# Windowed attention with a gated MLP: the first pair is transposed and brought out ahead of the branch, and the raw tiles of the third and fourth pair get places of their own

## The chip, the cores and the metric

One Trainium2 chip, one core of it. The metric is the time of the program on the device in microseconds (us), the median of several runs. Five engines work side by side, each through a list of its own in order: PE (TensorE, matrix products and transposes), DVE (VectorE), ACT (ScalarE), POOL (GpSimd) and SP (SyncE, which here issues nearly all DMAs). They wait for each other by semaphores.

## What is computed

q, k and v are float32 of shape 4 x 8 x 768 x 64 (batches, heads, positions, head size). Each head does attention in a band: a position sees the `n_sink` = 4 first positions and the last `window` = 128. The result, 4 x 768 x 512, goes through an MLP with a convolution over three positions and a gate; its weights come as 64-bit floats.

```python
scores = scale * np.matmul(q, k.transpose(0, 1, 3, 2))
keep = is_sink | in_window
scores = np.where(keep, scores, -1000000000.0)
a = np.exp(scores - np.max(scores, axis=-1, keepdims=True))
a = a / (np.sum(a, axis=-1, keepdims=True) + 1e-09)
x = np.matmul(a, v)                      # then heads side by side: 768 x 512
h = np.maximum(x @ w_in, 0.0)
conv_out = sum(conv_w[k] * hp[:, k:k + S, :] for k in range(3))   # hp: h, padded
out = h / (1.0 + np.exp(-conv_out)) @ w_out
```

## The kernel before

**The start.** SP loads the two scalars and the first four raw tiles: q and k of the first half (three tiles of 128 positions) of pair 0 and pair 1 (`raw`, L401). A *pair* is two heads, whose head sizes fill the 128 rows; there are 16 pairs, `g` 0 to 15, four a batch. DVE works out from the scalars whether band and sinks fit the fast path (`flag`, L874 to L876) and makes mask pieces (L896 to L902). All engines then load the flag and branch (L904, L906): `banded` if it is 1, `general` if not. Here it is 1.

**In the branch.** DVE makes the masks `m0`, `w1` and `w2` (L470 to L478), POOL fills zeros, the sinks' place `vs` and small tiles. Then a loop runs over steps: for the first batch all four pairs' first halves, then all second halves (24 steps of one query tile each), then pair by pair. In a step, PE multiplies the queries `X` with the keys `kk`/`kks` of the tile and its neighbour (`sc`, L378), DVE adds the mask and reduces (L577), ACT takes the exponent (L580), DVE sums and inverts (L583, L584), POOL scales (L586), PE transposes the result (L603), ACT copies it out (`pT`, L605), and PE multiplies with v (`px`, L655).

**Pairs of the first batch** come in plain float32: `prep32` has PE transpose a raw tile of q or k (`trq`, `trk`, L357) and ACT bring it out: q twice with `headscale` into `X`, k once into `kks` (L288), sinks beside it (L366). The four buffers `raw` are used in turn; `fetch` asks for the next load only when a transpose has been asked for, so that the load of pair 2's q goes where pair 0's q was.

**The weights** (`wi_0r` and so on, 512 KB each) come in the same loop: ACT starts with a scaled copy of the high words (`stm`, L118), DVE puts the bits together (L121 to L123), POOL and DVE split the result in a high and a low part (L130, L131). `WHEN` says at which step each is due; three buffers hold raw weights. From step 12 on, the MLP's products (`ph` L204, `po` L239) are laid between the steps.

The order on each engine is fixed ahead of the run by a scheduler from priorities and waits. SP's list is in order too, so a DMA that waits for its buffer holds back those behind it.

## Time and profile before

| | |
|---|---|
| median of 3 runs | 475.0 us (472.65 to 475.37) |
| the profiled execution | 473.48 us |
| its span, first to last instruction | 471.8 us |
| PE busy | 444.6 us (94%) |
| DVE busy | 339.0 us (72%) |
| ACT busy | 321.3 us (68%) |
| POOL busy | 281.3 us (60%) |
| chain that ended last | PE 75%, DVE 11%, ACT 4%, POOL 3%, DMA 2% |

The shares are averages over stages with different limits, so they are read by stages below. A row of the timeline gives start and duration in us, then engine, line, operation, what is written and read, and the count of merged instructions; in square brackets stands how long the engine was idle before it and what ended the wait. Issues of DMAs on SP show the time the issue took, not the flight.

### The profile page before, as it was taken

The page shows a single profiled execution, that of the slowest core. Times are in us where ns is not written, and L with a number is a line of the kernel's source. Part 1 is how long each engine was busy: PE and PEld are TensorE (multiplying, and loading weights), DVE is VectorE, ACT ScalarE, POOL GpSimd, SP SyncE. Part 2 cuts the span into 40 slices and gives each one's busy share as a digit, 9 for nine tenths or more (in the row PEclk, how much of TensorE's full clock was granted, in tenths as well). Part 3 has the DMA queues.
Part 4 walks back from the last instruction along what each step waited for, and adds up shares of the span by engine and source line. Part 5 has one row for each costly group of instructions (what it writes and reads, how often), then busy time and mean ns, then how long its engine had stood idle before and what let it go on. Part 6 is the DMA issues. An engine that isn't in the chain of part 4 may idle for free.

```text
span 471.8 us, 10560 instructions
## 1 busy us (share of the span) xinstructions
PE 444.6 (94%) x3181; PEld 388.3 (82%) x3181; DVE 339.0 (72%) x1190; ACT 321.3 (68%) x1027; POOL 281.3 (60%) x557
## 2 busy tenths in 40 slices
...
GB/s 140 219 229 251 183 201 107 81 199 203 167 153 179 137 175 68 161 146 133 61 192 81 166 119 134 143 120 124 71 141 15 46 1 46 0 23 24 24 24 53
DMA packets 105851, 55.91 MB, mean 119 GB/s; under 512 B 83072, under 2 KB 98712, under 8 KB 105784
## 3 DMA queue, kind: packets, MB, share of 16 engines
...
q10 hardware_dynamic: 144, 0.13, 0.1%
...
## 4 chain that ended last, share of the span: by engine, by line
PE 75%; DVE 11%; ACT 4%; POOL 3%; DMA 2%; issue 2%; DVEq 0%; POOLq 0%; ACTq 0%
PE ph L204 26%; PE po L239 25%; PE px L655 7%; PE sc L382 3%; PE sc L381 3%; PE pts L617 3%; PE px L678 2%; DVE stm L122 2%; PE tq L305 1%; PE tk L331 1%; DVE stm L123 1%; DMA kk<-bk 1%; DMA raw<-in_q_dram 1%; DVE roomH L577 1%; DVE roomL L577 1%
## 5 line engine op out<-in xcount | busy, mean ns | idle before, releaser
L239 PE MATMUL po<-woH,g 128*128 128x512 f32 x384 | 138.2, 405 | 1.5 <-POOL g L226 0.8
L204 PE MATMUL ph<-xH,wiH 128*128 128x258 f32 (+1 forms) x384 | 110.7, 288 | 0.0
L204 PE MATMUL ph<-xL,wiH 128*128 128x258 f32 (+1 forms) x384 | 109.6, 286 | 0.0
L204 PE MATMUL ph<-xH,wiL 128*128 128x258 f32 (+1 forms) x384 | 109.1, 284 | 0.0
L226 POOL TENSOR_SCALAR g<-t 128x256 fp32r<-128x256 f32 x94 | 44.3, 472 | 74.5 <-DVE t L219 50.6
L586 POOL TENSOR_SCALAR pe<-pe,sm 128x132 f32<-128x132 f32 (+1 forms) x144 | 62.8, 447 | 37.7 <-DVE sm L584 19.2
L239 PEld LDWEIGHTS po<-woH,g 128*128 128x128 f32 x384 | 69.4, 189 | 13.2 <-POOL g L226 1.7
L227 POOL TENSOR_TENSOR g<-t,g 128x256 fp32r<-128x256 f32 x94 | 74.5, 793 | 5.8
L239 PE MATMUL po<-woL,g 128*128 128x512 f32 x192 | 76.1, 396 | 0.0
L216 DVE SCALAR_TENSOR_TENSOR t<-hb,cw,t 128x256 f32<-128x256 f32 x96 | 53.8, 560 | 29.4 <-ACT t L215 28.9
L204 PEld LDWEIGHTS ph<-xH,wiL 128*128 128x128 f32 x384 | 72.8, 190 | 2.2
L204 PEld LDWEIGHTS ph<-xH,wiH 128*128 128x128 f32 x384 | 72.7, 189 | 2.0
L204 PEld LDWEIGHTS ph<-xL,wiH 128*128 128x128 f32 x384 | 72.7, 189 | 1.6
L580 ACT ACTIVATE pe<-pe,sm 128x132 f32<-128x132 f32 (+1 forms) x144 | 58.2, 406 | 14.4 <-DVE sm L577 12.8
L218 ACT ACTIVATE t<-t 128x256 f32<-128x256 f32 x96 | 40.1, 418 | 36.3 <-DVE t L217 35.9
L219 DVE SCALAR_TENSOR_TENSOR t<-t,hb 128x256 f32<-128x256 f32 x96 | 48.3, 504 | 15.1 <-ACT t L218 14.3
L215 ACT ACTIVATE t<-hb,cw 128x256 f32<-128x256 f32 x96 | 49.0, 511 | 12.4 <-POOL g L227 10.1
L217 DVE SCALAR_TENSOR_TENSOR t<-hb,cw,t 128x256 f32<-128x256 f32 x96 | 54.4, 567 | 4.0 <-POOL pe L586 0.5
L211 ACT ACTIVATE hb<-ph 128x258 f32<-128x258 f32 (+1 forms) x96 | 36.8, 384 | 17.4 <-PE ph L204 13.9
L577 DVE CUSTOM_DVE_ANT_0 pe<-sc,m 128x132 f32<-128x132 f32 (+1 forms) x144 | 39.8, 287 | 7.7 <-PE sc L382 6.9
L381 PE MATMUL sc<-kk,X 128*128 128x260 f32 (+1 forms) x144 | 42.3, 304 | 1.5 <-issue 1.1
L655 PE MATMUL px<-pT,vraw 128*64 128x128 f32 (+1 forms) x512 | 43.0, 317 | 0.0
...
## 6 DMA issues: line engine op xcount, KB each, us to landing
...
```

The lines of the kernel that those rows point to most:

```text
L204: self.latest = nc.tensor.matmul(u.h[:, 0:W], w[:, cc, ff * P:(ff + 1) * P], x[:, cc, t0:t1], start=(i == 0), stop=(i == len(prods) - 1))
L215: nc.scalar.mul(a, prev, cw[:, 0, ff:ff + 1])
L216: nc.vector.scalar_tensor_tensor(out=e, in0=this, scalar=cw[:, 1, ff:ff + 1], in1=a, op0=ALU.mult, op1=ALU.add)
L217: nc.vector.scalar_tensor_tensor(out=a, in0=nxt, scalar=cw[:, 2, ff:ff + 1], in1=e, op0=ALU.mult, op1=ALU.add)
L219: nc.vector.scalar_tensor_tensor(out=a, in0=e, scalar=1.0, in1=this, op0=ALU.add, op1=ALU.mult)
L227: nc.gpsimd.tensor_tensor(out=u.g[:, 1], in0=a, in1=f(u.g[:, 0]), op=ALU.subtract)
L239: ins = nc.tensor.matmul(po[:, 0:c.DM], u.g[:, a, tt * P:(tt + 1) * P], w[:, ff, :], start=(ff == 0 and i == 0), stop=(ff == NFF - 1 and i ...
L381: self.c.pin(self.nc.tensor.matmul(pc, X[:, j, u, :], kk[:, j, lo:hi], start=True, stop=False))
L577: nc.vector.tensor_tensor_reduce(out=pe[:, j, cols], in0=pc[:, P - at:SW][:, cols], in1=mk, op0=ALU.add, op1=ALU.min, scale=1.0, scalar=3. ...
L580: exp = nc.scalar.activation(pe[:, j, cols], pe[:, j, cols], AF.Exp, bias=sm[:, j:j + 1], scale=-1.0, accum_out=sm[:, 2 + 2 * j:3 + 2 * j])
L586: nc.gpsimd.tensor_scalar(pe[:, j, cols], pe[:, j, cols], sm[:, 8 + j:9 + j], 1.0, ALU.mult, ALU.mult)
L655: ins = nc.tensor.matmul(px[h][D * j:D * j + D, P * at:P * at + n], s.v[:, j, kt, :], pT, start=(h not in open_), stop=False, skip_group_c ...
```

## The change

Ahead of the branch: ACT, not SP, issues the loads of k of pairs 0 and 1. DVE clears a small tile `still`; PE runs six products of it (`WAKE`), transposes k and q of pair 0, and runs three more products (`IDLE`) behind them. ACT brings the transposes out into `kk0` and `X0`, which take the places of a raw v tile and of pair 0's raw tiles. The flag is worked out with two instructions on DVE and one on POOL; the exponent table is loaded by an instruction on `still`. Masks move: `sk` and `prv` to POOL, `m0` ahead of the branch, and the wide parts of `w1` and `w2` to POOL.

In the branch: `prep(0)` is gone. `homes` are eight places for raw tiles, four of them in a part of `kks[0]` that the plain pairs don't use; they hold q and k of the third and fourth pair (`g` 2 and 3). `fetch` is limited to `2 * n + 8`. The first v has a place of its own (`v0`). At step 3 POOL clears `zeros`, SP copies pair 0's third key tile from `kk0` into `kks`, and ACT its sinks. Transposes of pair 1 follow the first scores, its evacuation the first exponent. The rest is the same work.

```diff
@@ -30,0 +31 @@
+PRE = 4
@@ -36,0 +38,2 @@
+WAKE = 6
+IDLE = 3
@@ -120 +123 @@
-            follow(self.c, first, self.c.exps[-2], "late")
+            follow(self.c, first, self.c.exps[-2 if len(self.c.exps) > 4 else -1], "late")
@@ -357 +360,3 @@
-                c.pin(nc.tensor.transpose(pt[:, t, :], s.raw[nm, half][:, t].rearrange("p a d -> p (a d)"), c.ident))
+                ins = c.pin(nc.tensor.transpose(pt[:, t, :], s.raw[nm, half][:, t].rearrange("p a d -> p (a d)"), c.ident))
+                if g == 1 and half == 0:
+                    follow(c, ins, c.scored, "scores first")
@@ -361 +366,3 @@
-                    self.evac(s.X[half][:, j], pt, c.headscale[:, j:j + 1])
+                    ins = self.evac(s.X[half][:, j], pt, c.headscale[:, j:j + 1])
+                    if g == 1 and half == 0:
+                        follow(c, ins, c.exps[0], "exponents first")
@@ -378 +385 @@
-                self.c.pin(self.nc.tensor.matmul(pc, X[:, j, u, :], kk[:, lo:hi], start=True, stop=True))
+                self.c.scored = self.c.pin(self.nc.tensor.matmul(pc, X[:, j, u, :], kk[:, lo:hi], start=True, stop=True))
@@ -393,2 +400,3 @@
-def load(c, g, nm, t, lo, hi):
-
+def load(c, g, nm, t, lo, hi, by=None):
+
+    by = by or c.nc.sync
@@ -401 +409 @@
-        c.nc.sync.dma_start(t[:, j] if nm == "v" else t[:, :, j], both[j].rearrange("(t p) d -> p t d", p=P)[:, lo:hi])
+        by.dma_start(t[:, j] if nm == "v" else t[:, :, j], both[j].rearrange("(t p) d -> p t d", p=P)[:, lo:hi])
@@ -405 +413 @@
-def load_half(c, g, nm, half, slot):
+def load_half(c, g, nm, half, slot, by=None):
@@ -407 +415 @@
-    return load(c, g, nm, slot, n * half, n * half + n)
+    return load(c, g, nm, slot, n * half, n * half + n, by)
@@ -466 +473,0 @@
-    m0 = cp.tile([P, P], F32, name="m0")
@@ -469,3 +476 @@
-    before, sk, inw, prv = c.before, c.sk, c.inw, c.prv
-    nc.vector.tensor_tensor(out=m0, in0=inw, in1=sk, op=ALU.max)
-    nc.vector.tensor_scalar(m0, m0, -NEG, NEG, ALU.mult, ALU.add)
+    before, sk, inw, prv, m0 = c.before, c.sk, c.inw, c.prv, c.m0
@@ -473,2 +478,3 @@
-    nc.vector.tensor_scalar(w1[:, KW:SW], inw, -NEG, NEG, ALU.mult, ALU.add)
-    nc.vector.tensor_scalar(w1[:, 0:P], prv, -NEG, NEG, ALU.mult, ALU.add)
+    for w in wide:
+        nc.gpsimd.tensor_scalar(w[:, 0:P], prv, -NEG, NEG, ALU.mult, ALU.add)
+        masks = nc.gpsimd.tensor_scalar(w[:, KW:SW], inw, -NEG, NEG, ALU.mult, ALU.add)
@@ -477,2 +483 @@
-    nc.vector.tensor_copy(w2, w1)
-    masks = nc.vector.tensor_scalar(w2[:, P:KW], sk[:, 0:NS], -NEG, NEG, ALU.mult, ALU.add)
+    nc.vector.tensor_scalar(w2[:, P:KW], sk[:, 0:NS], -NEG, NEG, ALU.mult, ALU.add)
@@ -489 +494,2 @@
-            nc.vector.tensor_tensor(out=mk[:, NS:KW], in0=w[:, 0:P], in1=w[:, KW:SW], op=ALU.min)
+            ins = nc.vector.tensor_tensor(out=mk[:, NS:KW], in0=w[:, 0:P], in1=w[:, KW:SW], op=ALU.min)
+            follow(c, ins, c.turned, "late")
@@ -493 +498,0 @@
-    afterwards(nc.gpsimd.memset(A.zeros, 0.0))
@@ -494,0 +500,4 @@
+    rest = kks[0].rearrange("p a t k -> p (a t k)")[:, 2 * n0:2 * n0 + 12 * P]
+    rest = [rest[:, 3 * P * i:3 * P * i + 3 * P].rearrange("p (t a d) -> p t a d", a=2, d=D) for i in range(4)]
+    homes = c.raw + rest
+    v0 = m.room[1][:, 6 * SW:6 * SW + 3 * P].rearrange("p (j t d) -> p j t d", j=2, d=D)
@@ -517 +525,0 @@
-    st[0].v = c.v_raw[0]
@@ -524,5 +532,3 @@
-    for i, (g, nm, half) in enumerate(queue[0:RAWB]):
-        st[g].raw[nm, half] = c.raw[i]
-    asked = [RAWB]
-
-    free = [0]
+    for i, (g, nm, half) in enumerate(queue[0:PRE]):
+        st[g].raw[nm, half] = homes[i]
+    asked, turned, free = [PRE], [0], [0]
@@ -531 +537,2 @@
-        free[0] += 1
+        free[0] += turned[0] not in range(RAWB, len(homes))
+        turned[0] += 1
@@ -536,0 +544,4 @@
+            if asked[0] < len(homes):
+                st[g].raw[nm, half] = load_half(c, g, nm, half, homes[asked[0]])
+                asked[0] += 1
+                continue
@@ -711,3 +722,3 @@
-    for x in prep(0):
-        x()
-    load_v(c, 0, 0, 0, T // 2)
+    st[0].X[0], st[0].kk, st[0].plain, st[0].v = c.X0, c.kk0, True, v0
+    for nm in "qk":
+        ahead()
@@ -714,0 +726,4 @@
+    fetch(RAWB + 2)
+    load(c, 0, "v", v0, 0, T // 2)
+    fetch(RAWB + 4)
+    m.fetch(2)
@@ -716,2 +730,0 @@
-    fetch()
-    m.fetch(2)
@@ -744 +757 @@
-                fetch()
+                fetch(2 * n + 8 if n < NPAIR else len(queue))
@@ -747 +760,2 @@
-                    nc.sync.dma_start(f(vsr).rearrange("p u n -> p (u n)")[:, x:x + half_row], A.zeros[0:3 * SR, 0:half_row])
+                    ins = nc.sync.dma_start(f(vsr).rearrange("p u n -> p (u n)")[:, x:x + half_row], A.zeros[0:3 * SR, 0:half_row])
+                    follow(c, ins, c.exps[-1], "late")
@@ -756,0 +771,6 @@
+        if i == T // 2:
+            follow(c, nc.gpsimd.memset(A.zeros, 0.0), c.exps[-1], "late")
+            u = T // 2 - 1
+            nc.sync.dma_start(kks[0][:, 0, u], c.kk0[:, u])
+            sinks = nc.scalar.copy(kks[0][:, 0, u + 1:T, P:KW], c.kk0[:, 0:1, 0:NS].to_broadcast([P, T - u - 1, NS]))
+            follow(c, sinks, c.exps[-1], "late")
@@ -870,2 +890,7 @@
-    for i in range(RAWB):
-        load_half(c, i // 2, "qk"[i % 2], 0, c.raw[i])
+    c.X0 = c.whole[0].rearrange("p t a d -> p (t a d)").rearrange("p (a t k) -> p a t k", a=2, t=T // 2)
+    flat = c.v_raw[0].rearrange("p j t d -> p (j t d)")
+    c.kk0 = flat[:, 0:T // 2 * KW].rearrange("p (t k) -> p t k", k=KW)
+    still = flat[:, T // 2 * KW:T // 2 * KW + 3 * D]
+    for i in range(PRE):
+        load_half(c, i // 2, "qk"[i % 2], 0, c.raw[i], nc.scalar if i % 2 else nc.sync)
+    nc.vector.memset(still, 0.0)
@@ -874,4 +899,5 @@
-    nc.vector.tensor_scalar(fl[:, 0:1], c.wnv, 1.0, None, ALU.is_ge)
-    nc.vector.scalar_tensor_tensor(out=fl[:, 1:2], in0=c.wnv, scalar=float(P), in1=fl[:, 0:1], op0=ALU.is_le, op1=ALU.mult)
-    flagged = nc.vector.scalar_tensor_tensor(out=flag, in0=c.nsv[0:1], scalar=float(NS), in1=fl[0:1, 1:2], op0=ALU.is_le, op1=ALU.mult)
-    nc.scalar.activation(fl[:, 0:1], fl[:, 1:2], AF.Exp)
+    ended = con.tile([P, 1], F32, name="ended")
+    nc.scalar.activation(ended, still[:, 0:1], AF.Exp)
+    nc.gpsimd.tensor_scalar(fl[:, 0:1], c.nsv, float(NS), None, ALU.is_le)
+    nc.vector.scalar_tensor_tensor(out=fl[:, 1:2], in0=c.wnv, scalar=float(P + 1), in1=c.wnv, op0=ALU.subtract, op1=ALU.mult)
+    flagged = nc.vector.scalar_tensor_tensor(out=flag, in0=fl[0:1, 1:2], scalar=-float(P), in1=fl[0:1, 0:1], op0=ALU.is_le, op1=ALU.mult)
@@ -893 +918,0 @@
-    wprev = con.tile([P, 1], F32, name="wprev")
@@ -898,2 +923,3 @@
-    c.tc = tc
-    follow(c, nc.vector.tensor_scalar(c.sk, C, c.nsv, None, ALU.is_lt), flagged, "flag first")
+    c.m0 = con.tile([P, P], F32, name="m0")
+    nc.gpsimd.tensor_scalar(c.sk, C, c.nsv, 1.0, ALU.is_lt, ALU.mult)
+    nc.gpsimd.tensor_scalar(c.prv, R, c.wnv, -float(P), ALU.subtract, ALU.is_lt)
@@ -901,2 +927,22 @@
-    follow(c, nc.vector.tensor_scalar(wprev, c.wnv, -float(P), None, ALU.add), flagged, "flag first")
-    nc.vector.tensor_scalar(c.prv, R, wprev, None, ALU.is_lt)
+    nc.vector.tensor_tensor(out=c.m0, in0=c.inw, in1=c.sk, op=ALU.max)
+    nc.vector.tensor_scalar(c.m0, c.m0, -NEG, NEG, ALU.mult, ALU.add)
+    with tc.tile_pool(name="wake", bufs=1, space=PSUM) as wake:
+        turn = wake.tile([P, 3 * D], F32, name="turn")
+
+        def idle(n, last=None):
+            for i in range(n):
+                ins = nc.tensor.matmul(turn, still[:, 0:P], still, start=True, stop=True)
+                if last is not None:
+                    follow(c, ins, last, "in its place")
+
+        idle(WAKE)
+        pts = {}
+        for i, nm in ((1, "k"), (0, "q")):
+            pts[nm] = wake.tile([P, T // 2, P], F32, name=f"first{nm}")
+            for t in range(T // 2):
+                last = nc.tensor.transpose(pts[nm][:, t, :], c.raw[i][:, t].rearrange("p a d -> p (a d)"), c.ident)
+        idle(IDLE, last)
+        nc.scalar.mul(c.kk0[:, :, 0:P], pts["k"], 1.0)
+        for j in range(2):
+            nc.scalar.mul(c.X0[:, j], pts["q"], c.headscale[:, j:j + 1])
+        nc.scalar.copy(c.kk0[:, :, P:KW], c.kk0[:, 0:1, 0:NS].to_broadcast([P, T // 2, NS]))
```

Three places of the order show what moved. First SP, behind the branch. Before (`vraw_69` is v of pair 0, `raw_67` and `raw_68` are the raw buffers, here for pairs 2 and 3, `kks_160` holds the place of the sinks):

```order
L401 DMA vraw_69<-in_v_dram 128x3x64 x2
L106 DMA wi_0r<-in_moe_w_in_dram 128x1024
L401 DMA raw_67<-in_q_dram 128x3x64 x2
L401 DMA raw_67<-in_k_dram 128x3x64 x2
L106 DMA wi_1r<-in_moe_w_in_dram 128x1024
L401 DMA raw_68<-in_q_dram 128x3x64
L423 DMA kks_160<-in_v_dram 4x4x64 x6
L401 DMA raw_68<-in_q_dram 128x3x64
L401 DMA raw_68<-in_k_dram 128x3x64 x2
L401 DMA vraw_70<-in_v_dram 128x3x64 x2
```

After the change (`roomL` is the place of v of pair 0, `kks_185` holds the places of pairs 2 and 3):

```order
L109 DMA wi_0r<-in_moe_w_in_dram 128x1024
L409 DMA roomL<-in_v_dram 128x3x64 x2
L109 DMA wi_1r<-in_moe_w_in_dram 128x1024
L409 DMA kks_185<-in_q_dram 128x3x64 x2
L409 DMA kks_185<-in_k_dram 128x3x64 x2
L409 DMA kks_185<-in_q_dram 128x3x64 x2
L409 DMA kks_185<-in_k_dram 128x3x64 x2
L431 DMA kks_186<-in_v_dram 4x4x64 x6
L409 DMA vraw_70<-in_v_dram 128x3x64 x2
L774 DMA kks_185<-vraw_69 128x132
```

The first two weights stand ahead of pair 2's q and k, and pair 3's loads now stand ahead of the six small sink loads.

Second ACT. Before, from the branch on (`X_182` and `kks_159<-trk_185` are pair 0, `X_224` is pair 1, `X_321` is pair 2; `roomH` and `roomL` are score tiles of even and odd pairs):

```order
L288 ACTIVATE X_182<-trq_178,headscale 128x384 x2
L288 ACTIVATE kks_159<-trk_185 128x3x128
L366 COPY kks_159<-kks_159 128x6x4
L288 ACTIVATE X_224<-trq_220,headscale 128x384 x2
L580 ACTIVATE roomH,sm_163<-roomH,sm_163 128x128
L288 ACTIVATE kks_159<-trk_243 128x3x128
L580 ACTIVATE roomH,sm_163<-roomH,sm_163 128x128
L366 COPY kks_159<-kks_159 128x6x4
L118 ACTIVATE stm_256<-wi_0r 128x512
L580 ACTIVATE roomH,sm_164<-roomH,sm_164 128x260
L288 ACTIVATE X_321<-trq_317,headscale 128x384 x2
L580 ACTIVATE roomH,sm_164<-roomH,sm_164 128x260
```

After (`X_241` is pair 1, `X_337` is pair 2):

```order
L591 ACTIVATE roomH,sm_189<-roomH,sm_189 128x128 x2
L291 ACTIVATE X_241<-trq_237,headscale 128x384 x2
L591 ACTIVATE roomH,sm_190<-roomH,sm_190 128x260
L291 ACTIVATE kks_185<-trk_260 128x3x128
L591 ACTIVATE roomH,sm_190<-roomH,sm_190 128x260
L373 COPY kks_185<-kks_185 128x6x4
L616 COPY pT_0_258<-pts 128x256
L121 ACTIVATE stm_269<-wi_0r 128x512
L591 ACTIVATE roomH,sm_191<-roomH,sm_191 128x260 x2
L591 ACTIVATE roomL,sm_192<-roomL,sm_192 128x128
L291 ACTIVATE X_337<-trq_333,headscale 128x384 x2
```

Pair 0's evacuations are gone from this stretch, and pair 2's stands behind four exponents more.

Third PE, from its first instruction (`turn` is what the idle products write):

```order
L934 MATMUL turn<-vraw_69 128x192 x6
L943 MATMUL firstk<-ident,raw_67 128x128 x3
L943 MATMUL firstq<-ident,raw_67 128x128 x3
L934 MATMUL turn<-vraw_69 128x192 x3
L950 TENSOR_LOAD flag
L952 COMPARE_AND_BRANCH
L385 MATMUL sc_0_0_225<-vraw_69,raw_67 128x128
L385 MATMUL sc_0_1_226<-vraw_69,raw_67 128x128
L360 MATMUL trq_237<-ident,raw_68 128x128 x3
```

Before, this list began behind the branch, with the transposes of q of pair 0; now the first scores stand there.

## Rows read from the trace of the kernel before

**Rows 1.** Windows: busy us (x instructions) of each engine, granted clock, DMA share, GB/s.

```profile
5.00:10.00 5.00, 2.51 (x11) 2.14 (x12) 3.75 (x19) 1.90 (x6) 2.04 (x17) 1.00 0.84 173
...
10.00:15.30 5.30, 4.92 (x18) 3.75 (x18) 1.94 (x11) 4.31 (x13) 1.77 (x3) 1.00 0.92 263
...
15.30:25.40 10.10, 7.83 (x46) 5.64 (x44) 9.27 (x40) 10.10 (x37) 6.53 (x12) 1.00 0.83 212
...
25.40:85.00 59.60, 53.25 (x406) 43.41 (x406) 58.57 (x164) 46.82 (x137) 38.97 (x54) 1.00 0.67 185
...
85.00:130.00 45.00, 41.25 (x319) 35.86 (x319) 33.52 (x145) 35.54 (x125) 27.62 (x55) 1.00 0.70 172
...
130.00:455.00 325.00, 324.59 (x2344) 289.69 (x2341) 225.50 (x797) 216.68 (x704) 200.71 (x404) 1.00 0.39 98
```

**Rows 2.** Timeline of ACT, 7 to 24 us; in brackets idle time and releaser.

```profile
7.90 1.05 ACT L288 ACTIVATE X<-trq,headscale 128x384 f32<-128x384 f32 x2 [1.93 <-DVE roomH L474]
...
9.95 1.05 ACT L288 ACTIVATE X<-trq,headscale 128x384 f32<-128x384 f32 x2 [0.37 <-PE trq L357]
...
11.04 0.40 ACT L580 ACTIVATE roomH<-roomH,sm 128x128 f32<-128x128 f32 x1
...
12.89 0.66 ACT L118 ACTIVATE stm<-wi_0r 128x512 f32<-128x512 f32 x1 [0.48 <-DMA wi_0r<-in_moe_w_in_dram]
...
14.51 1.05 ACT L288 ACTIVATE X<-trq,headscale 128x384 f32<-128x384 f32 x2 [0.47 <-PE trq L357]
...
23.43 0.68 ACT L118 ACTIVATE stm<-wi_2r 128x512 f32<-128x512 f32 x1
```

**Rows 3.** Chain of waits of 0 to 130 us: start, duration, what.

```profile
8.27 4.86 DMA raw<-in_q_dram
```

**Rows 4.** Timeline of 0 to 14 us, all engines; in brackets idle time before.

```profile
0.80 1.28 ACT L877 ACT_TABLE_LOAD   x1 [0.80 <-PEq L927]
...
5.77 0.15 DVE L876 SCALAR_TENSOR_TENSOR flag<-sc_v,fl 1x1 int32<-1x1 f32 x1
...
6.62 0.11 POOL L567 MEMSET roomH<- 128x8 f32 x1 [4.70 <-DVE wprev L901]
...
6.91 0.88 PE L357 MATMUL trq<-ident,raw 128*128 128x128 f32 x3 [6.91 <-SPq L938]
```

**Rows 5.** Timeline of the DMA issues on SP: start, duration, line, transfer, count.

```profile
1.71 0.96 SPq L401 DMA_DIRECT2D raw<-in_q_dram  x2
...
7.68 0.42 SPq L106 DMA_DIRECT2D wi_0r<-in_moe_w_in_dram  x1
...
8.27 0.90 SPq L401 DMA_DIRECT2D raw<-in_q_dram  x2
...
18.04 0.48 SPq L106 DMA_DIRECT2D wi_2r<-in_moe_w_in_dram  x1
```

**Rows 6.** DMA view of 0 to 8 us: GB/s in 40 slices.

```profile
GB/s 0 0 0 0 0 0 0 0 0 1 1 1 1 1 1 1 2 44 105 138 148 193 261 278 270 233 252 245 247 251 250 214 164 242 227 99 50 27 49 209
```

**Rows 7.** Timeline of PE: transposes of k.

```profile
7.57 0.85 PE L357 MATMUL trk<-ident,raw 128*128 128x128 f32 x3
...
15.44 0.49 PE L357 MATMUL trk<-ident,raw 128*128 128x128 f32 x3
```

**Rows 8.** Timeline of POOL, 8 to 14 us.

```profile
8.97 0.76 POOL L493 MEMSET roomH<- 128x792 f32 x1 [1.31 <-DVE roomH L478]
...
9.67 1.38 POOL L496 MEMSET kks<- 96x1536 f32 x1
...
13.97 0.38 POOL L586 TENSOR_SCALAR roomH<-roomH,sm 128x128 f32<-128x128 f32 x1 [2.92 <-DVE sm L584]
```

**Rows 9.** Timeline of DVE, 10 to 26 us.

```profile
10.71 0.29 DVE L577 CUSTOM_DVE_ANT_0 roomH<-sc,m 128x128 f32<-128x128 f32 x1 [1.60 <-PE sc L378]
...
15.31 0.43 DVE L577 CUSTOM_DVE_ANT_0 roomH<-sc,roomH 128x260 f32<-128x260 f32 x1 [1.22 <-PE sc L378]
...
25.46 0.42 DVE L121 TENSOR_SCALAR stm<-stm 128x512 int32<-128x512 int32 x1
```

2 lines of the change are left out of this document (1 added, 1 removed).

## The prediction

> **What bounds the kernel now.** I read the table by stages first, because the shares over the whole span hide which engine is short in which stage. From 130 to 455 us PE is busy in 324.59 of 325.00 us: nothing can be won there, and whatever happens before it only moves it. From 25.4 to 85 us DVE is the full engine, 58.57 of 59.60 us, while PE still has 6.35 us free. From 15.3 to 25.4 us it is ACT, 10.10 of 10.10 us. From 10 to 15.3 us no compute engine but PE is near full (ACT 4.31, DVE 1.94 of 5.30), and from 85 to 130 us PE lacks 3.75 of 45.00 us [rows 1].
>
> So the program is a relay: start-up, then ACT, then DVE, then PE. A microsecond won at the start reaches the end only if the engine that is full next gets its work earlier too. The reader should see in the rows of ACT how the start goes: after the branch it first brings out pair 0 (from 7.90), waits 0.37 us for PE, brings out pair 1's q from 9.95, runs its first exponent at 11.04, and starts the evacuation of pair 2's q at 14.51 [rows 2]. The chain of waits says what that last one hung on: the load of pair 2's q, issued at 8.27, when PE had read the buffer's former content, and 4.86 us under way [rows 3].
>
> **What the change does to the start.** Pair 0's transposes and evacuations go ahead of the branch, where ACT has nothing but its table load (0.80 to 2.08) and PE nothing until 6.91 [rows 4]. They need k and q of pair 0. Before, SP issues q at 1.71, 0.96 us for its two DMAs, and k after it; data flow from 3.4 us on, 1.7 us after the first issue [rows 5, 6]. Now ACT issues k itself, from 0.80 on. It pays four issues, two of them for pair 1, at SP's price of 0.48 each: 1.9 us, so its table load ends at 0.80 + 1.9 + 1.28 = 4.0, before any data can be used; the issues cost nothing as long as k isn't landed by then. With 1.7 us from issue to flow, k and q of pair 0 (384 KB) flow from 2.5 us; before, the first 384 KB took from 3.4 to 5.4 us (ten slices of 0.2 us, 193 GB/s on average) [rows 6]. That gives 4.5 us, and 4.8 with some time for the completion. If k came no sooner than before, it would be 5.5.
>
> The Trainium skill (DMA: Bandwidth & Descriptors, Issuing engines are not separate DMA queues) speaks against a gain here: whatever engine starts a DMA, it runs on the same 16 DMA engines, and a second issuer saves only issue time. The rows agree with the premise, but here issue time is the larger part: about 1.0 us of issues per 192 KB against about 0.8 us of flow at 250 GB/s. By the skill's rule taken strictly, all that follows would start 0.7 us later; the sum below is made without it, and the case counts to the first rival.
>
> From 4.8 us: six transposes at 0.22 us (0.66 for three, the spacing of the two groups at 6.91 and 7.57 [rows 4, 7], at the slow rate, see below) to about 6.3; k's evacuation lies beside q's transposes; two evacuations of q take 1.05 us [rows 2], to 7.3. Then ACT loads the flag and branches. The flag is written at 5.92, the first POOL instruction behind the branch is at 6.62 and PE's at 6.91: 0.7 to 1.0 us [rows 4]. ACT is in the branch at 8.2, PE before that, since its three idle products and the flag are done by then; the two first scores and DVE's first reduction fit in the same time. **ACT's first exponent starts at 8.3 instead of 11.04.** Bounds: 7.6 if the data land by 4.2, 9.2 if they land as before.
>
> The flag itself loses two DVE instructions and gains one on POOL: under 0.2 us, taken as nothing. The masks that move from DVE to POOL (four of 128x128, before the 1.38 us fill of the sinks' place on POOL [rows 8]) take about 0.4 us each there by the nearest row, a softmax scaling of that size, so POOL is free at about 11, when the first softmax tile is ready for it at about 10; PE's two transposes of that tile and pT_0 on ACT, about 12, hide that. Without that cover it would be 1 us on DVE and ACT. The 0.76 us fill of zeros [rows 8] now stands on POOL behind the second scaling and waits for a late exponent; what is behind it there is the split of the first weights and the third softmax tile, both needed later than 15 us; 0 to 0.8 us, taken as 0.
>
> **ACT's stage.** From 7.90 to the start of the work on weight wi_2r at 23.43, ACT works 15.53 us less three waits (0.37, 0.48 and 0.47): 14.2 us [rows 2]. Of it pair 0's evacuations and its copy of sinks go ahead of the branch (7.90 to 9.58, which is 9.95 less the wait: 1.7 us), and one copy of 0.2 us comes in: 12.7 us. Starting at 8.3 and without a wait it would be at wi_2r at 21.0. But the order has pair 2's evacuation behind 5.6 us of these (two evacuations, kk, two copies, one weight, seven exponents at 0.40 us and, the wider ones, 0.1 more), at 13.9, and its data are not there: q of pair 2 is issued behind wi_0r, v and now wi_1r, at about 8.6, no earlier than the 8.27 of before [rows 5]. Having its own place frees it from PE, not from the queue. 512 KB more are ahead of it, 1.9 us at the 263 GB/s of 10 to 15.3 us [rows 1], while the first loads ahead of it end about 0.9 sooner; it landed at 13.13 before (8.27 + 4.86) [rows 3], so I take 14.2, with PE's three transposes 14.6. **ACT reaches wi_2r at 14.6 + 7.1 = 21.7 instead of 23.43.** wi_2r itself is no hindrance: issued at 18.04 before [rows 5], and at about 17.5 now that pair 3's loads don't stand behind the small sink loads; 4.5 us of flight, which the ACT queue covers nearly. Were it not covered, 22.2.
>
> **DVE's stage.** DVE starts on wi_2r when ACT has done its part of 0.66 us [rows 2]: 22.4 instead of 25.46 [rows 9]. It can: its work up to there is 1.94 + 9.27 us [rows 1], and it has 14 us from its first reduction at 8.0, instead of 10.71 with 1.60 and 1.22 us of waiting behind it [rows 9]. But two reductions of pair 2 at 0.43 us, which before were done by then, stand behind wi_2r now. 3.1 - 0.9 = 2.2 us are left, and DVE has only 1.03 us of idle time from there to 85 us, so it hands this on. I take 0.2 off for the longer list of DMAs and the new order. **2.0 us** reach the stage of PE and so the end. Less is possible (0.6: first exponent at 9.2 and wi_2r late), more too (3: X2 without a wait).
>
> The rest of the program holds the same instructions in another order on every engine; in 85 to 130 us, where PE lacks 3.75 us [rows 1], this can give or take. I take 0, with 1.5 us either way. The zero rows for vsr now wait on SP for the exponent of the twelfth step; behind them stand loads of v, k and weights for later steps. Nothing.
>
> **The sum.** The profiled execution takes 473.48 us, 471.8 of span and 1.7 around it: 471.5 with 2.0 us less. It is 1.5 below the median of 475.0, which the runs shown spread around by 2.7 us. Predicted median: **473.0 us**.
>
> **Rivals.** *The start is given back.* ACT waits for pair 2's data and weights anyway, and the wait only moves: for it speaks that q of pair 2 isn't issued earlier; against it that 1.7 us of ACT's work are gone for good and that ACT has no idle time in 15.3 to 25.4 us. It gives 0 to 0.8 us: 474.2 to 475, say 474.7.
>
> *PE's clock stays low.* PE works at about half rate at first: trq at 6.91 and trk at 7.57 take 0.88 and 0.85 us for three, trk at 15.44 takes 0.49 [rows 4, 7], although the granted clock reads 1.00, which is 2.4 GHz, in all stretches from 5 us on [rows 1]; by their durations the first ones go at the lower level, 1.2 GHz. The rate rose after PE had been busy in 2.51 of 5.00 and then in 4.92 of 5.30 us. The idle products are to bring this about before; but the transposes that filled PE after 6.91 are now partly gone, and between the last idle product and the first scores PE waits for ACT. If the clock rises only when PE gets dense, at about 25 us, PE's 7.83 busy us of 15.3 to 25.4 would become up to 15 in 10 us of room; some of that is hidden, say 3.5 us are lost against a gain of 2: 476.5, slower. It decides from the point where transposes still take over 400 ns at 20 us. The Trainium skill (TensorE: Matmul & The Clock Gate, Part 1) has the rule behind it: the throttled state is the default and activity releases it.
>
> *The start is worth more.* The clock is up at 7 us, the loads come smoothly, ACT never waits (0.7 us more), the DVE's idle time of 4.2 us in 10 to 25.4 us [rows 1] shrinks, and half of the 3.75 us in 85 to 130 goes: 4.5 us, 470.5. Against it: DVE depends on ACT there, whose sum is above.
>
> **Chances.** Forecast (1 to 3.3 us less): 0.50. Given back: 0.18. Clock low, or a loss by order of that size: 0.13. More: 0.19. Range: 469.6, between the larger gain and its own spread of about 1 us, to 476.3, which leaves half of the slow case outside; about 0.2 is left out. The forecast's own range is 471.5 to 474.3. One per cent, about what a measurement of this kernel can tell from no change, is 4.75 us. Faster by more needs the upper half of the last rival and the low side of the runs: 0.15. Slower by more needs over twice the price of the clock: 0.05. Same: 0.80.
>
> **What would show it.** Right: ACT's first exponent by 8.7 us; pair 2's evacuation at 14 to 15 and waiting for PE or the load; wi_2r on ACT at 21 to 22.5; DVE full from 22 on; PE's stage begins 1.5 to 2.5 us earlier, with 0.4 us or less idle after it. Wrong: the first exponent after 9.5 (loads not earlier), transposes over 400 ns after 16 us (the clock), a DVE that waits for PE or DMA between 25 and 85 us, or a PE that lacks over 5 us between 85 and 130.

## The result, and the profile after

The changed kernel takes 479.51 us (five runs, 478.89 to 480.91) against 475.36 us of the kernel before on the same chip: 1.0101 times as long, 95% interval 1.0068 to 1.0133. The prediction, 473.0 us and a range up to 476.3, had the wrong sign. The profiled execution takes 478.96 us with a span of 477.2, 5.4 us more than before.

The table by stages of the changed kernel; the columns are stretch, length, then busy us (x instructions) of PE, PE's weight loads, DVE, ACT and POOL, granted clock, DMA share, GB/s:

```profile
5.00:10.00 5.00, 3.75 (x22) 2.91 (x22) 2.77 (x15) 2.25 (x7) 4.09 (x21) 1.00 0.72 187
10.00:15.30 5.30, 3.24 (x16) 2.02 (x14) 3.79 (x19) 5.08 (x18) 3.22 (x8) 0.97 0.84 218
15.30:25.40 10.10, 7.87 (x48) 6.12 (x50) 6.44 (x28) 8.44 (x28) 5.49 (x11) 0.84 0.70 188
25.40:85.00 59.60, 50.37 (x368) 39.81 (x363) 55.20 (x155) 43.39 (x126) 37.90 (x51) 0.97 0.66 186
85.00:130.00 45.00, 43.06 (x322) 37.70 (x321) 33.77 (x137) 36.60 (x124) 26.98 (x52) 1.00 0.66 160
130.00:455.00 325.00, 323.73 (x2342) 287.58 (x2341) 226.11 (x812) 217.05 (x711) 200.63 (x407) 1.00 0.40 101
```

Beside [rows 1]: from 10 to 15.3 us DVE does twice the work (3.79 for 1.94), as the earlier start should bring. From 15.3 to 25.4 us ACT, full before, is idle for 1.66 us, and DVE for 3.66 where it was idle for 0.83. From 25.4 to 85 us DVE, which the prediction took to be full, waits 4.40 us (1.03 before), and PE waits 9.23 us (6.35). PE's time from 10 us to the end splits the loss: 443.7 us busy and 23.5 idle in the span after, 442.1 and 19.7 before (PE's busy total of the page less that of the first 10 us, and the rest of the span). 3.8 us of the 5.4 are waiting, 1.6 us are longer work; the granted clock is 0.97, 0.84 and 0.97 in the three stages from 10 to 85 us, where it was 1.00 [rows 1].

The start, in the timeline of the changed kernel (start, duration, engine, line, operation, idle time before it):

```profile
0.80 2.08 ACTq L409 DMA_DIRECT2D raw<-in_k_dram  x4
...
2.91 1.28 ACT L900 ACT_TABLE_LOAD   x1 [2.91 <-issue]
...
5.40 0.52 PE L943 MATMUL firstk<-ident,raw 128*128 128x128 f32 x3 [0.24 <-DMA raw<-in_k_dram]
...
6.07 0.74 POOL L924 TENSOR_SCALAR vraw<-vraw,sc_v 128x128 f32<-128x128 f32 x1
...
6.68 0.52 PE L943 MATMUL firstq<-ident,raw 128*128 128x128 f32 x3 [0.76 <-DMA raw<-in_q_dram]
6.79 0.86 POOL L925 TENSOR_SCALAR vraw<-vraw,sc_v 128x128 f32<-128x128 f32 x1
...
7.94 0.30 POOL L479 TENSOR_SCALAR roomH<-vraw 128x128 f32<-128x128 f32 x1
...
9.11 0.29 DVE L588 CUSTOM_DVE_ANT_0 roomH<-sc,m 128x128 f32<-128x128 f32 x1 [0.58 <-POOL sm L511]
...
9.50 0.40 ACT L591 ACTIVATE roomH<-roomH,sm 128x128 f32<-128x128 f32 x1 [1.16 <-DVE sm L588]
...
13.07 0.68 ACT L121 ACTIVATE stm<-wi_0r 128x512 f32<-128x512 f32 x1
...
15.70 0.87 PE L360 MATMUL trq<-ident,kks 128*128 128x128 f32 x3 [1.80 <-DMA kks<-in_q_dram]
...
16.61 1.05 ACT L291 ACTIVATE X<-trq,headscale 128x384 f32<-128x384 f32 x2 [1.49 <-PE trq L360]
...
18.02 0.68 ACT L121 ACTIVATE stm<-wi_1r 128x512 f32<-128x512 f32 x1
...
23.98 0.68 ACT L121 ACTIVATE stm<-wi_2r 128x512 f32<-128x512 f32 x1 [0.36 <-DMA wi_2r<-in_moe_w_in_dram]
```

The first exponent comes at 9.50 us (11.04 before [rows 2]). Then PE waits 1.80 us for q of pair 2, ACT 1.49 us for PE, and pair 2's evacuation starts at 16.61 instead of 14.51 [rows 2]. The queue says why; issues on SP:

```profile
8.92 0.90 SPq L409 DMA_DIRECT2D kks<-in_q_dram  x2
...
11.07 3.62 SPq L409 DMA_DIRECT2D kks<-in_q_dram  x2
...
19.84 0.58 SPq L109 DMA_DIRECT2D wi_2r<-in_moe_w_in_dram  x1
```

and the chain of waits (start, duration):

```profile
9.40 6.16 DMA kks<-in_q_dram
```

Pair 2's q is issued from 8.92 on (8.27 before [rows 5]) and landed at 15.56; before, [rows 3] had it landed at 13.13. The two issues of pair 3's q take 3.62 us, and wi_2r, behind them, is issued at 19.84 (18.04 before).

How far the softmax has come is read by counting DVE's masked reductions (L577 before, L588 after). Start of the n-th, in us, from the timelines; the last three columns are kernels of the experiments below:

| n | before | after | after, pair 2's loads first, order held | one index put back | before, order of after from about 25 us |
|---|---|---|---|---|---|
| 8 | 17.50 | 14.28 | 14.28 | 16.34 | 16.49 |
| 12 | 21.20 | 21.10 | 18.16 | 20.38 | 20.34 |
| 16 | 25.10 | 30.33 | 28.52 | 23.45 | 24.26 |
| 24 | 37.55 | 39.42 | 38.33 | 35.58 | 40.12 |
| 60 | 115.35 | 119.09 | 118.61 | 113.61 | 119.85 |

At the eighth reduction the change is 3.2 us ahead, at the twelfth the lead is gone, at the sixteenth it is 5.2 us behind. DVE's rows show what it did in between. Before:

```profile
24.66 0.43 DVE L577 CUSTOM_DVE_ANT_0 roomH<-sc,roomH 128x260 f32<-128x260 f32 x1 [0.32 <-PE sc L378]
...
25.10 0.43 DVE L577 CUSTOM_DVE_ANT_0 roomH<-sc,roomH 128x260 f32<-128x260 f32 x1
...
25.91 0.85 DVE L122 SCALAR_TENSOR_TENSOR stm<-wi_2r,stm 128x512 int32<-128x512 int32 x1
...
28.73 0.68 DVE L122 SCALAR_TENSOR_TENSOR stm<-wi_3r,stm 128x512 int32<-128x512 int32 x1
```

After:

```profile
25.36 0.84 DVE L125 SCALAR_TENSOR_TENSOR stm<-wi_2r,stm 128x512 int32<-128x512 int32 x1
...
28.12 0.73 DVE L125 SCALAR_TENSOR_TENSOR stm<-wi_3r,stm 128x512 int32<-128x512 int32 x1
...
29.38 0.41 DVE L588 CUSTOM_DVE_ANT_0 roomH<-sc,roomH 128x260 f32<-128x260 f32 x1
...
30.33 0.41 DVE L588 CUSTOM_DVE_ANT_0 roomH<-sc,roomH 128x260 f32<-128x260 f32 x1
```

The weights are not late: wi_2r is 0.55 us earlier than before. The two wide reductions of pair 2 that stood ahead of it stand behind wi_2r and behind the start of wi_3r now. PE waits longer for DVE in this stage: its groups of 25.4 to 65 us (count, busy us and mean ns, idle us before them and releasers), before,

```profile
L378 PE MATMUL sc<-kks,X 128*128 128x260 f32 (+1 forms) x40 | 11.7, 386 | 0.5 <-DVE sm L577 0.5
```

and after:

```profile
L385 PE MATMUL sc<-kks,X 128*128 128x260 f32 (+1 forms) x44 | 13.3, 398 | 4.8 <-DVE sm L588 4.4 <-DMA vsr<-roomH 0.3
L614 PE MATMUL pts<-ident,roomH 128*128 128x128 f32 x18 | 3.9, 297 | 2.5 <-POOL roomH L597 2.3
```

The scores wait 4.4 us for DVE where they waited 0.5. Only 1.34 us of that come right behind the two late reductions (PE's scores at 29.86); the rest lies at five other places up to 62 us.

### The profile page after: what moved, and what is told of

Same layout as the page of the kernel before. It is cut to its first block, busy times and chain, and to the rows that moved or that the text cites. A ratio compares the mean times of both kernels' runs of the same rounds, so it can differ in the third digit from the quotient of the medians.

```text
span 477.2 us, 10660 instructions
## 1 busy us (share of the span) xinstructions
PE 451.3 (95%) x3199; PEld 392.2 (82%) x3199; DVE 337.8 (71%) x1184; ACT 321.8 (67%) x1028; POOL 284.6 (60%) x564
## 4 chain that ended last, share of the span: by engine, by line
PE 78%; POOL 6%; DVE 6%; DMA 3%; issue 2%; ACT 1%; SPq 0%; POOLq 0%; DVEq 0%; ACTq 0%
PE ph L207 27%; PE po L242 26%; PE px L666 8%; PE sc L389 3%; PE sc L388 3%; PE pts L628 3%; PE px L689 2%; POOL roomL L597 2%; PE tq L308 2%; PE tk L334 2%; POOL roomH L597 1%; DMA kks<-in_q_dram 1%; PE sc L385 1%; POOL g L229 1%; DMA wo0r<-in_moe_w_out_dram 1%
## 5 line engine op out<-in xcount | busy, mean ns | idle before, releaser
L207 PE MATMUL ph<-xH,wiH 128*128 128x258 f32 (+1 forms) x384 | 112.4, 293 | 0.0
L207 PE MATMUL ph<-xH,wiL 128*128 128x258 f32 (+1 forms) x384 | 110.3, 287 | 0.0
L597 POOL TENSOR_SCALAR pe<-pe,sm 128x132 f32<-128x132 f32 (+1 forms) x144 | 65.6, 466 | 38.5 <-DVE sm L595 20.7
L230 POOL TENSOR_TENSOR g<-t,g 128x256 fp32r<-128x256 f32 x94 | 72.4, 771 | 6.1
L587 DVE COPY_PREDICATED sc<-before,sc 128x128 f32<-128x128 int32 x120 | 32.1, 288 | 16.9 <-PE sc L389 16.1
L666 PE MATMUL px<-pT,vraw 128*64 128x128 f32 (+1 forms) x492 | 41.5, 318 | 0.2 <-ACT pT L616 0.2
L388 PE MATMUL sc<-kk,X 128*128 128x260 f32 (+1 forms) x144 | 40.6, 295 | 0.3 <-PE po L242 0.2
```

What stands on the lines that cost most here:

```text
L207: self.latest = nc.tensor.matmul(u.h[:, 0:W], w[:, cc, ff * P:(ff + 1) * P], x[:, cc, t0:t1], start=(i == 0), stop=(i == len(prods) - 1))
L230: nc.gpsimd.tensor_tensor(out=u.g[:, 1], in0=a, in1=f(u.g[:, 0]), op=ALU.subtract)
L388: self.c.pin(self.nc.tensor.matmul(pc, X[:, j, u, :], kk[:, j, lo:hi], start=True, stop=False))
L597: nc.gpsimd.tensor_scalar(pe[:, j, cols], pe[:, j, cols], sm[:, 8 + j:9 + j], 1.0, ALU.mult, ALU.mult)
L666: ins = nc.tensor.matmul(px[h][D * j:D * j + D, P * at:P * at + n], s.v[:, j, kt, :], pT, start=(h not in open_), stop=False, skip_group_c ...
```

## Experiments

Three explanations stood against each other: the order on the engines that the scheduler dealt for the changed program is worse; PE's clock, which the granted clock shows below 1.00 in three stages, costs the time; pair 2's q, landed later, costs it. A fourth was that the new places and the load order do harm by themselves. Ratios are to the kernel before in the same batch on the same chip (medians 473.2 to 475.0 us).

**Fewer idle products ahead of the first transposes.**

```diff
-WAKE = 6
+WAKE = 4
```

> The changed kernel with four idle products ahead of the first transposes instead of six; every other instruction stands in the same order on all five engines. Two products are 0.3 to 0.6 us of PE before its data land, so nothing should move if the loss has another cause than the idle products: 479 to 480, ratio to the kernel before 1.008 to 1.012. If the clock is the cause (the granted clock of 0.66 in 15 to 20 us) and hangs on these products, the time goes up by 1 us or more, the transposes of the first pair take over 0.6 us for three.

```diff
-WAKE = 6
+WAKE = 3
```

> The changed kernel with three idle products instead of six. Against the run with four, the program differs by one idle product of some 0.15 to 0.45 us at the start, but the scheduler gives out another order for most of the program (some 430 rows of PE, 330 of DVE and 260 of ACT stand elsewhere). Theory order (the static order that the changed start draws costs the 3 us in 25 to 85 us): the time differs from that with four products by 1 us or more, either way, and the windows from 25 us on differ. Theory load (the loss is pair 2's q landing at 15.6 instead of 13.1, and the rest of the program only carries it): the time is that with four products, 479 to 480.

Four give 479.23 us, 1.0099 (1.0061 to 1.0137), with the order unchanged: as the changed kernel. Three give 477.40 us, 1.0056 (1.0028 to 1.0083, runs from 474.3 to 479.9). One product of 0.64 us less (PE's six, four and three products take 3.98, 2.93 and 2.29 us) made the scheduler deal another order on every engine, and the median moved by about 2 us, though the two intervals overlap. The start ran otherwise too: the first three transposes take 0.87 us with three products and 0.52 with four. So this pair of runs doesn't tell order from start; it only shows that a small change of the start brings another order with it.

**Pair 2's loads ahead of v and wi_1r, order dealt anew.**

```diff
+def ordered(c, ins):
+    if getattr(c, "second", None) is not None:
+        c.tc.add_manual_dep(ins.ins, c.second.ins.name, mybir.DependencyInfo(mybir.DependencyClass.NoSync,
+                                                                             mybir.DependencyReason.DATA), reason="order")
+    return ins
...
+    c.second = c.loaded
     load(c, 0, "v", v0, 0, T // 2)
-    fetch(RAWB + 4)
     m.fetch(2)
+    c.second = c.lastw
+    fetch(RAWB + 4)
```

> The changed kernel with the loads of pair 2 issued behind weight wi_0r and ahead of v of pair 0 and wi_1r, by dependencies that only set the order. Theory load: pair 2's q lands 2 to 2.5 us earlier (13 to 13.5), its evacuation starts by 14.2, the wait of PE and DVE at 14 to 17 us goes, and 2 to 2.5 us of the loss come back: 476.5 to 477.5. Theory order: the start improves in the same way, but the end comes out anywhere within 3 us, not in step with the first 25 us. Theory clock: with PE's wait gone the granted clock of 15 to 20 us returns to 0.9 or more, and a further 1 us comes back.

478.87 us, 1.0077 (1.0051 to 1.0103). Pair 2's evacuation starts at 12.81 without a wait, 3.8 us sooner, and hardly anything comes of it; in this order wi_0r is on ACT at 14.51, 1.4 us later than in the changed kernel.

**The places alone.** The kernel before with `homes`, which free pair 3's loads from PE:

```diff
+    rest = [rest[:, 3 * P * i:3 * P * i + 3 * P].rearrange("p (t a d) -> p t a d", a=2, d=D) for i in range(4)]
+    homes = c.raw + rest
...
-        free[0] += 1
+        free[0] += turned[0] not in range(RAWB, len(homes))
```

> The kernel before with only the second part of the change: raw tiles of pairs 3 and 4 (the third and fourth in order) have places of their own, nothing ahead of the branch. If the places and what they do to SP's queue (more loads ahead of the weights, issues that wait for the load eight earlier) carry the loss, it shows here: 477 to 480. If the loss comes from the new start or from the wait for q behind wi_1r, this kernel stays at 474 to 476; q of that pair can then be issued without waiting for PE's transposes.

480.12 us, 1.0102 (1.0057 to 1.0147). Loads of later pairs now stand ahead of the weights, and ACT starts on wi_1r only at 22.45. So I added the change's order of loads and its limit:

```diff
+    fetch(RAWB + 2)
+    load_v(c, 0, 0, 0, T // 2)
+    fetch(RAWB + 4)
...
-                fetch()
+                fetch(2 * n + 8 if n < NPAIR else len(queue))
```

> The kernel before with the places for the raw tiles of the third and fourth pair, and, unlike the run with the places alone, with the change's order of the first loads and its limit on how far loads run ahead (so that wi_1r and wi_2r are not behind loads of later pairs). Nothing ahead of the branch. If the places make the scheduler deal the bad order: 477.5 to 480, with reductions behind the narrowing of wi_2r and wi_3r as in the changed kernel. If the earlier start as such makes it: 474 to 476.

477.89 us, 1.0071 (1.0044 to 1.0098). Both are slower than before without the new start; their orders were dealt anew as well, so this doesn't yet tell places from order.

**Orders held.** To tell order from work, a table of places fixes each engine's list: dependences that order two neighbours of one engine without a wait.

```diff
+    for engine, places in PLACES.items():
+        traced = [i for i in nc.cur_bb.bb.instructions if str(i.engine) == "EngineType." + engine
+                  and not any(x in type(i).__name__ for x in ("Boundary", "Release"))]
+        for a, b in zip(places, places[1:]):
+            c.tc.add_manual_dep(traced[b], traced[a].name, mybir.DependencyInfo(mybir.DependencyClass.NoSync,
+                                                                               mybir.DependencyReason.DATA), reason="order")
```

First the kernel before, held in the order of the changed one from about 25 us on (from place 45 of PE, 44 of DVE, 36 of ACT, 35 of POOL and SP):

> The kernel before, whose instructions from the same places on are held in the order in which the changed kernel has them; its start is untouched, no new places, no idle products. Theory order: 477 to 481, with spells of granted clock at 0.5 between 30 and 70 us, as with the changed kernel. Theory load: 473.5 to 476, as the kernel before, since its loads come as before.

479.83 us, 1.0134 (1.0096 to 1.0172): without a line of the change, its order from there on costs more than the whole change does (by the medians; the intervals overlap). The granted clock is 1.00 in every stage up to 455 us, PE is busy for 442.2 us from 10 us on, as before, and idle for 26.1 instead of 19.7: all of it is waiting, at the same two places as in the changed kernel (groups of 25.4 to 65 us):

```profile
L532 PE MATMUL sc<-kks,X 128*128 128x260 f32 (+1 forms) x40 | 12.1, 397 | 5.0 <-DVE sm L731 4.9
...
L757 PE MATMUL pts<-ident,roomH 128*128 128x128 f32 x18 | 3.8, 292 | 3.8 <-POOL roomH L740 2.4 <-ACT pT L759 1.3
```

Yet in this kernel the two wide reductions of pair 2 still stand ahead of wi_2r, as before the change; DVE:

```profile
23.82 0.43 DVE L731 CUSTOM_DVE_ANT_0 roomH<-sc,roomH 128x260 f32<-128x260 f32 x1 [0.32 <-PE sc L532]
...
24.26 0.43 DVE L731 CUSTOM_DVE_ANT_0 roomH<-sc,roomH 128x260 f32<-128x260 f32 x1
...
25.07 0.85 DVE L276 SCALAR_TENSOR_TENSOR stm<-wi_2r,stm 128x512 int32<-128x512 int32 x1
```

So their place is not needed for the loss. It comes behind them: at the sixteenth reduction this kernel is 0.8 us ahead of before, at the 24th 2.6 us and at the 60th 4.5 us behind. From 39 to 110 us DVE goes through nearly the same waits as in the changed kernel, about 0.7 us later. An example, first from the changed kernel, then from this one:

```profile
70.88 0.96 DVE L134 TENSOR_TENSOR wiL<-stm,wiH 128x512 fp32r<-128x512 f32 x1 [1.23 <-POOL wiH L133]
```

```profile
71.61 0.69 DVE L285 TENSOR_TENSOR wiL<-stm,wiH 128x512 fp32r<-128x512 f32 x1 [1.22 <-POOL wiH L284]
```

Then the changed kernel in the order of before, first from about 25 us on (from place 50 of DVE, 40 of ACT and POOL, 100 of PE, 36 of SP), then from the branch on (20, 20, 26, 50, 28):

> The changed kernel, whose instructions from about 25 us on (from the 100th of PE, the 50th of DVE, the 40th of ACT and of POOL and the 36th of SP in the branch) are held by order-only dependencies in the order in which the kernel before has them; the start is that of the change. Theory order: the time is that of the kernel before or a little less, 472 to 475, and no spell of low granted clock after 30 us. Theory load (late loads and weights of the new start are carried to the end): 477.5 to 480, whatever the order. Theory clock (the start alone pulls the granted clock down at 15 to 19 us): 476 to 477, with the low spell at 15 to 19 still there.

> The changed kernel with its own start and its own loads, but all engines held in the order of the kernel before as soon as the branch allows it (from the 20th instruction of DVE and ACT, the 26th of POOL, the 50th of PE, the 28th of SP): the two wide reductions of pair 2 stand ahead of the narrowing of wi_2r again, which they do not in the run that was held from 25 us on only. Theory order: the 2.4 us that were lost between 25 and 34 us in that run are not lost, 473 to 475, as before or 1 us above. Theory load: the wait for pair 2's q (1.8 us) and the later wi_2r remain and keep it at 475.5 to 477.

477.04 us, 1.0074 (1.0050 to 1.0098), and 475.89 us, 1.0030 (1.0010 to 1.0051). In the first the two wide reductions still stand behind wi_2r; DVE's rows, which now come in the order of before, are 0.6 us ahead of before at 24 us, 2.4 behind at 37 and 2.5 at 85. In the second the two stand ahead again, and the rows are 1.8 behind from 45 to 85 us: the place of the two is worth at most some 0.6 us in these traces. Held from the branch, most of the loss is gone, 3.4 us of it (1.0101 to 1.0030). With pair 2's loads ahead of v and wi_1r as well (`0-6 11 7-10` on SP; 0 is wi_0r, 1 to 4 are q and k of pair 2, 5 and 6 v, 11 wi_1r, 7 to 10 pair 3, 21 wi_2r):

> As the run before in this series (changed start, order of the kernel before on all engines), with q and k of pair 2 also issued ahead of v of pair 0 and of wi_1r. Both theories want this to be the best of all: 472 to 474 if the order and the load carry the whole loss, so that the earlier first exponent (9.5 instead of 11.0) can reach the end; it is the version that could beat the kernel before. If it stays above 475, something else in the new start costs time, such as the loads that now stand ahead of wi_2r.

475.13 us, 1.0024 (1.0006 to 1.0041). The early start has no gain in the order of before.

**Clock and loads with the changed kernel's own order held.** Eight idle products in PE's wait for pair 2's q:

```diff
+            for t in range(8 if (g, half, nm) == (2, 0, "q") else 0):
+                c.fill = getattr(c, "fill", []) + [c.pin(nc.tensor.matmul(pt[:, 0, :], c.ident, c.ident, start=True, stop=True)).ins]
```

> The changed kernel, every instruction held in its own order on all five engines, with eight idle products of 128x128 (about 0.2 us each) on PE ahead of the transposes of pair 2's q, where PE waits 1.8 us for that load. Nothing else moves. Theory clock: the granted clock stays at 1.00 over 15 to 19 us, where it read 0.50 to 0.78, PE's transposes there take 0.49 instead of 0.87 us, and 0.7 to 1.6 us come back: 477.5 to 478.5. If the low clock at 15 to 19 us is hidden behind other engines' work: 479 to 479.7, though the clock reads 1.00.

479.05 us, 1.0109 (1.0073 to 1.0145). In PE's timeline and in the windows:

```profile
13.75 1.95 PE L522 MATMUL trq<-ident 128*128 128x128 f32 x16
15.59 0.52 PE L524 MATMUL trq<-ident,kks 128*128 128x128 f32 x3
```

```profile
15.30:25.40 10.10, 8.42 (x64) 6.33 (x63) 6.67 (x27) 8.00 (x25) 6.69 (x12) 1.00 0.67 189
25.40:85.00 59.60, 49.05 (x356) 37.92 (x355) 55.05 (x158) 44.13 (x130) 38.20 (x50) 1.00 0.67 188
```

The transposes take 0.52 us instead of 0.87 and the clock stays at 1.00, but DVE idles as before the filling (55.05 busy against 55.20) and the time is the same within the intervals: the low clock was real, and no gain is seen from lifting it. The Trainium skill (TensorE: Matmul & The Clock Gate, Part 1) says that activity releases the throttled state; these rows agree with that, and yet the release brings nothing here that the runs can tell.

Only SP's places changed, pair 2's q and k ahead of v and wi_1r (`0-6 11 7-10` for `0 5-6 11 1-4 7-10`):

> The changed kernel, every instruction held in its own order on all five engines, but for one piece of SP's queue: q and k of pair 2 are issued ahead of v of pair 0 and of wi_1r. Theory load: pair 2's q lands at about 13.5 instead of 15.56, its evacuation on ACT starts at 14.7 to 15.2 instead of 16.6, and 1.5 us or more come back: 477 to 478. Theory order: the first 25 us get shorter by up to 1.5 us, but the time stays at 478.5 to 479.7, because the engines wait on each other later on.

478.34 us, 1.0102 (1.0068 to 1.0137). Pair 2's evacuation starts at 15.02 instead of 16.61, wi_2r at 22.71 instead of 23.98, the twelfth reduction at 18.16 instead of 21.10, and the sixteenth, behind the weights in the held order, at 28.52 (before: 25.10). The late load isn't what the time hangs on as long as that order stands.

**One stretch of the order.** The changed kernel's own order, but with that of before from about 17 to 38 us (DVE's places 20 to 71, PE 43 to 106, ACT 29 to 66, POOL 31 to 52):

> The changed kernel in its own order on all engines except one stretch: from the 20th to the 71st instruction of DVE (and the 43rd to 106th of PE, 29th to 66th of ACT, 31st to 52nd of POOL), about 17 to 38 us, the order of the kernel before holds. Theory order, at one place (the reductions of pairs 2 and 3 behind the narrowing of wi_2r and wi_3r): 476 to 477.5, DVE's third wide reduction of pair 2 ends by 29 us instead of 31.7. If the loss by order is spread over the whole of 25 to 130 us: 478 to 479.5.

479.64 us, 1.0116 (1.0089 to 1.0144): no gain, though the two reductions are at 24.10 and 24.53, ahead of wi_2r. Their place alone brings nothing back; at the seam of the two orders DVE waits 2.11 us for ACT and PE 1.79 us for DVE (34.91 and 35.65 us).

**Does any new order lose?** The kernel before with four small copies on ACT that nobody reads (and a POOL fill of the tile they use), which made the scheduler deal another order:

```diff
+    for i in range(4):
+        nc.scalar.mul(c.spare, c.spare, 1.0)
```

> The kernel before with nothing of the change: four copies of 128x64 on ACT at the start of the branch, 0.2 us each, which lead the scheduler to another order (some 360 rows of PE and 330 of DVE stand elsewhere). If the order of the kernel before is a good draw that any shift of the start loses: 477 to 480, more than the 0.8 us of the copies explain (474.8 to 475.8). If the order of the changed kernel is bad because of what the change does: 474.5 to 476.

474.57 us, 1.0008 (0.9993 to 1.0023). No: at least one other order is as good as that of before.

**Single lines put back.** The wide masks to DVE again, and, apart from that, the one index that the diff changes at the weights:

```diff
-        nc.gpsimd.tensor_scalar(w[:, 0:P], prv, -NEG, NEG, ALU.mult, ALU.add)
-        masks = nc.gpsimd.tensor_scalar(w[:, KW:SW], inw, -NEG, NEG, ALU.mult, ALU.add)
+        nc.vector.tensor_scalar(w[:, 0:P], prv, -NEG, NEG, ALU.mult, ALU.add)
+        masks = nc.vector.tensor_scalar(w[:, KW:SW], inw, -NEG, NEG, ALU.mult, ALU.add)
```

> The changed kernel with its four mask fills back on DVE, where the kernel before has them; 1.4 us more on DVE and 1.2 us less on POOL ahead of the first reduction, and another order behind it. If the masks on POOL (two of 0.75 us ahead of the branch, four in it) make the order bad or hold up the first reduction: 475 to 477. If not: 477.5 to 480.

```diff
-            follow(self.c, first, self.c.exps[-2 if len(self.c.exps) > 4 else -1], "late")
+            follow(self.c, first, self.c.exps[-2], "late")
```

> The changed kernel with one index put back: the first weights' narrowing follows the exponent before the last, not the last, as in the kernel before. It deals another order, in which both wide reductions of pair 2's second step stand ahead of the narrowing of wi_2r again. If it is this place that costs: 475.5 to 477. If the early start gets a worse order wherever it is dealt: 477.5 to 480.

Masks on DVE: 478.36 us, 1.0074 (1.0048 to 1.0101). The index: 474.49 us, 1.0000 (0.9983 to 1.0018); the loss is gone. The line sets behind which exponent the work on a weight may start, between two ACT instructions, so it moves the order and adds no wait of its own. ACT's timeline of this kernel:

```profile
11.33 0.67 ACT L121 ACTIVATE stm<-wi_0r 128x512 f32<-128x512 f32 x1
...
14.94 0.67 ACT L121 ACTIVATE stm<-wi_1r 128x512 f32<-128x512 f32 x1 [0.70 <-DMA wi_1r<-in_moe_w_in_dram]
...
16.39 1.03 ACT L291 ACTIVATE X<-trq,headscale 128x384 f32<-128x384 f32 x2
```

wi_0r goes 1.7 us earlier than in the changed kernel (13.07) and wi_1r 3.1 us earlier (18.02), ahead of pair 2's evacuation; exponents that the changed kernel ran ahead of its wait of 1.49 us for pair 2 now run in that time, and ACT, after a wait of 0.70 us for wi_1r, goes on to pair 2 at 16.39 without another. DVE is then ahead: the sixteenth reduction is at 23.45, and from 25.4 to 85 us it is nearly full again, 57.78 of 59.60, and PE's scores wait 1.6 us:

```profile
25.40:85.00 59.60, 54.51 (x399) 43.70 (x399) 57.78 (x159) 46.86 (x136) 38.86 (x52) 0.97 0.69 190
```

```profile
L385 PE MATMUL sc<-kks,X 128*128 128x260 f32 (+1 forms) x38 | 11.3, 388 | 1.6 <-DVE sm L588 1.4
```

Pair 2's q is as late here as in the changed kernel (16.39 against 16.61).

**What the start is worth, and a better kernel.** The kernel before in the order of the last one, held from just behind the branch:

> The kernel before, start and loads untouched, held from the 50th instruction of PE and the 25th of DVE and ACT on in the order that the changed kernel has with its one index put back. If the earlier start is worth the predicted 2 us in a suitable order: 476 to 477, 2 us above the 474.5 of the changed kernel in this order. If the start is given back: 474 to 475.5.

475.84 us, 1.0021 (0.9994 to 1.0048). Against 1.0000 the new start gives 1.0 us in this order, within both intervals; the two profiled executions are 2.3 us apart in span (474.3 and 472.0), one execution each. In the changed kernel's order it is 1.0101 against 1.0134, 1.6 us, within both intervals too; in the order of before it costs 1.4 us (1.0030 against 1). Two tries to use it: the order of before with pair 2's loads and the weights' early, and the order of the last kernel held, with SP's list wi_0r, q of pair 2, wi_1r, k of pair 2, v, wi_2r, then pair 3 (`0-2 11 3-6 21 7-10` on SP):

> The changed kernel held in the order of the kernel before, with pair 2's q and k issued right behind wi_0r, then wi_1r, v of pair 0 and wi_2r, ahead of pair 3 and of the small loads of sinks. If the start was given back at the wait for wi_2r (0.6 us on ACT at 23 us in the run without this) and at PE's waits: 472 to 473.5, faster than the kernel before. If the start is worth nothing even so: 474 to 475.5.

> The changed kernel with its one index put back, every instruction held in the order it then has, but for SP's queue: wi_0r, q of pair 2, wi_1r, k of pair 2, v of pair 0, wi_2r, then pair 3 as before. If the waits on the loads hold back the start's gain (2.15 us of PE at 13.4 to 15.6 for q of pair 2, 0.78 us of ACT at 23 us for wi_2r): q lands by 14, wi_2r's narrowing starts by 23, 472.5 to 473.7. If these waits are covered by other work: 474 to 475.

The first gives 475.48 us, 1.0024 (1.0004 to 1.0045). The second gives 472.73 us, 0.9948 (0.9927 to 0.9968), 2.5 us faster than before by that ratio, and 1.5% faster than the changed kernel (0.9948 / 1.0101). ACT's timeline:

```profile
15.66 1.04 ACT L451 ACTIVATE X<-trq,headscale 128x384 f32<-128x384 f32 x2
...
21.95 0.70 ACT L281 ACTIVATE stm<-wi_2r 128x512 f32<-128x512 f32 x1
```

wi_2r is on ACT at 21.95 (the prediction had said 21.7) with no wait, and from 15.3 to 25.4 us ACT works 9.85 and DVE 9.02 of 10.10 us. Since only SP's places differ from the kernel with the index put back, the loads in front are worth about 2.5 us by the ratios (0.9948 against 1.0000; their intervals don't overlap) and 1.8 us by the medians (472.73 and 474.49, on two chips). The trace shows a lead of DVE's rows of 1.3 us up to 31 us, of which 0.2 us are left from 79 to 113 us; from 118 us on this execution is 1.2 us behind. It is the slowest of the twelve, so where the others gain is not shown.

**All runs together.** DVE's idle time between 10 and 130 us orders nearly all of the profiled executions:

| kernel | DVE idle, 10 to 130 us | its span | ratio of medians |
|---|---|---|---|
| loads in front, held | 16.4 | 472.6 | 0.9948 |
| one index put back | 16.6 | 472.0 | 1.0000 |
| before | 16.7 | 471.8 | 1 |
| changed, order of before from the branch | 18.8 | 474.3 | 1.0030 |
| before, dealt anew | 19.5 | 474.1 | 1.0008 |
| changed | 20.8 | 477.2 | 1.0101 |
| changed, PE's wait filled | 20.9 | 477.7 | 1.0109 |
| before, order of changed from about 25 us | 21.2 | 478.3 | 1.0134 |
| places only | 26.4 | 479.3 | 1.0102 |

Over the twenty kernels (18 experiments, before and changed) the correlation of the two middle columns is 0.90, and 0.94 without the one with places only; its slope there is 1.1 us of span per us of idle DVE. That is a relation of 20 traces, not a proof of cause, and it doesn't separate the first three rows. The first row's profiled execution takes 474.45 us; that kernel's runs begin at 471.81 us.

## Why the prediction was wrong

**What bounds the kernel** was read rightly: a relay from ACT to DVE to PE, with the end fixed by what PE has waited for until 130 us. PE's stage from 130 us is as full as before (323.73 of 325.00). What was missed is what the new order does to the stage in which DVE is full.

**The failed step** is the sentence "The rest of the program holds the same instructions in another order on every engine [...] I take 0, with 1.5 us either way". That term alone is +6.3 us in the kernel before held in the new order from about 25 us on (0.0134 of the 473.2 us of its batch), and 3.4 us with the new start (1.0101 in its own order, 1.0030 in that of before). Both are more than twice the 1.5 us. That the two differ fits an order serving worse under a start for which it wasn't dealt; no run tests this. The prediction even names a place, "two reductions of pair 2 at 0.43 us, which before were done by then, stand behind wi_2r now", priced at their own 0.9 us. They do come 5 us later (24.66 to 29.38), and PE waits 1.34 us right behind them; but the loss doesn't hang on them, since it is as large with both ahead of wi_2r (1.0134 and 1.0116). It is spread over many waits of 25 to 130 us: of PE for DVE (4.4 us in the changed kernel, 4.9 in the kernel before held in its order, instead of 0.5) and for POOL's scalings, and of DVE for weights from ACT and POOL.

**"DVE has only 1.03 us of idle time from there to 85 us, so it hands this on"** failed by the same cause. DVE was that full in the order of before; in the new order it waits for 4.40 us there, mostly for POOL and ACT.

**The start**, step by step. The issues on ACT (2.08 us said 1.9) and its table load (ends 4.19, said 4.0) were right. k and q were said to land at 4.8; k's transposes start at 5.40 and q's, which waited 0.76 us for the data, at 6.68. Data flow from 2.2 us on (3.4 before [rows 6]), but at 28 to 111 GB/s up to 4 us, where the sum had taken 193; the four raw tiles are in at about 7 us in both kernels. The Trainium skill (DMA: Bandwidth & Descriptors, Issuing engines are not separate DMA queues), which the prediction had set against its own sum, says that a second issuer saves only issue time; these times agree with it. The clock was up by then in this execution (0.52 us for three transposes; the sum had 0.66). Pair 0 was out 1.0 us later than said (8.34 for 7.3). POOL's two mask tiles ahead of the branch, for which the sum had no term, took 0.74 and 0.86 us, so that POOL was in the branch only at 7.59; of the four fills there, priced at 0.4 each, each took 0.30, and DVE's first reduction waited 0.58 us for a small fill of `sm` behind them. The first exponent is at 9.50 (said 8.3, bounds 7.6 to 9.2): 1.5 us won, not 2.7.

**Pair 2's q** was said to be issued at 8.6 and landed at 14.2, with the evacuation at 14.6; it was issued at 8.92, landed at 15.56, and the evacuation started at 16.61. 1 MB of weights and 192 KB of v were issued ahead of it, and 192 KB of k right behind it; which of them slowed it wasn't tried. The issues of pair 3's q behind them took 3.62 us. **wi_2r** was said to be issued at 17.5 and on ACT at 21.7; it was 19.84 and 23.98. So from these two steps alone the 2.0 us of the sum were gone: ACT reached wi_2r 0.55 us later than before [rows 2]; that DVE was at it at 24.89 and not at 25.46 [rows 9] is only because its two reductions had gone behind. That is the mechanism of the rival "the start is given back", which ended at 474.7: in the order of before from the branch on, the changed kernel is at 1.0030, 1.4 us more than before. The order cost the rest.

**The rival "PE's clock stays low"** had the sign and 476.5 us. The clock did fall, though not as it said: the first transposes ran at the higher of the two levels, and it fell after PE's wait of 1.80 us (0.87 us for three transposes where 0.52 is had at full clock). But held up by idle products it gave nothing back (1.0109 against 1.0101, intervals of some 0.0035 either way): no price is seen, and one of 3.5 us is outside these intervals. **"The start is worth more"** was said to need loads that come smoothly and an ACT that never waits. The kernel with the loads in front is nearer to that and is faster by 2.5 us, but not by the 4.5 us said there.

**The signs to look for** pointed the right way: the first exponent came at the bound of 9.5, and DVE waited between 25 and 85 us, though for POOL (2.1 us) and ACT (1.4) and only 0.5 for PE, not for PE or DMA as the sign had it. PE lacked only 1.94 us from 85 to 130 us.

**What stays open:** which trait of the new order costs how much. The two reductions behind the weights are ruled out as the main part; which of the later waits are the main part isn't tried. That the index put back works through the filled wait (wi_0r and wi_1r ahead of pair 2) is argued from the timeline; the index changes the order elsewhere too, and the two weren't tried apart.
